# Gated attention and MLP mixer on one core: the spreading of head rows and the split of the output projection rewritten, selection matrices built on another engine

## The chip, the cores and the metric

The kernel runs on one core of one Trainium2 chip. Its time is device microseconds (us) from the start to the end of one launch. The profile is one execution of the same program on that core; its span runs from the first instruction to the last. Engines are named as in the profile: PE is the matrix engine (PEld its weight loads), DVE the vector engine, ACT the scalar engine, POOL is GpSimd, and SP is the engine whose queue issues the large transfers (DMA).

## The reference

Eight sequences with one new token each (x is 8 x 448, bf16). Two branches are mixed by a gate, out = g * a + (1 - g) * b:

```python
g = sigmoid((x * gate_w).sum(-1, keepdims=True))
# a: 16 query heads of 256 over 8 cached KV heads, last 1024 positions of 4096
q = (x @ wq).reshape(B, Sq, Hq, Dh).transpose(0, 2, 1, 3)
scores = einsum("bhqd,bhkd->bhqk", q, k) * (Dh ** -0.5)
o = einsum("bhqk,bhkd->bhqd", softmax(scores), v)
a = o.transpose(0, 2, 1, 3).reshape(B, Sq, Hq * Dh) @ wo      # (8, 4096) @ (4096, 448)
# b: an MLP
h = gelu(layernorm(x) @ w1 + b1)
b = h @ w2 + b2
```

The caches that are read (1024 positions of K and of V, 8 heads, 8 sequences) are 67 MB, the weights some 11 MB.

## The kernel before, in words

All large transfers go through one SP queue into a ring of 9 slots of 2 MB (`RING`, `pump`, `done`). Their order is a fixed plan: wq, the first K block, w1, w2, then K and V blocks by turns, the last two V blocks, and at the end wo in four pieces: quarters 0 and 1 in one (1792 KB), quarter 2 (896 KB), six eighths of quarter 3 (672 KB), and the rest of it (224 KB). A slot is loaded again when its reader is done. The order of instructions on each engine is the order in which the Python code writes them; semaphores between engines are placed automatically, tile by tile.

**Start.** POOL fills constants, the last of them `qw` (line 290, a memset of 128 x 5120). DVE builds small selection matrices out of the identity matrix `ident`, among them `pick` (lines 282 to 289): four copies of 128 x 128. Then the norm and the gate are computed (`norm_and_gate`; POOL fills `each` at line 337), then the query (`query`): wq matmuls into `Sq`, ACT scales them to bf16, PE transposes them, DVE arranges them into `qd`, PE multiplies by the four matrices in `pick` (line 393) into a two-bank PSUM tile `qp`, and ACT (line 406) and DVE (line 408) by turns copy blocks of 32 rows of `qp` into `qw`: ACT the half j = 0, DVE the half j = 1, for each of four row blocks.

**Loop.** A unit u (16 of them) is one sequence and four KV heads. DVE transposes the K block in two halves (line 351), PE makes scores (lines 417 and 423), DVE takes maxima, ACT exponentiates, DVE transposes the result back, PE multiplies by V (line 495), ACT and DVE pick out the own heads, and `finish(u)` (lines 525 and 528) puts the gated attention output, transposed, into columns of `oT`. In the iterations u = 12, 13 and 14, `keep_clock(idle, 2, 1)` (line 636) adds three matmuls whose result nobody reads: one in f32 and two in bf16, each 512 columns wide.

**End.** `oT` holds, for partition p, head h, half j and batch b, the attention output at head dimension 2p + j. The projection wants on each partition eight consecutive rows of wo, so `spread_rows` regroups: PE multiplies four strided column picks of `ident` (32 columns each) by four groups of heads, 16 matmuls of 64 columns, each into its own 32 rows of the PSUM tile `pp` (line 660), and DVE copies the whole of `pp` into `oP` (line 667). `oP` is cut into four quarters q of 8 blocks j. The product with wo is accumulated over q and j. Quarters 0 and 1 are done in whole rows of 448 columns (`project_whole`, line 673) into `A_all`, which already holds the MLP part (`begin`); ACT copies `A_all` to SBUF (`save_whole`, line 683). Quarters 2 and 3 are done in two halves of 224 columns (`project`, line 701) into two PSUM tiles that sit on different rows (0 to 7 and 32 to 39). Between them, `add_whole` (line 687) adds the saved rows to the halves by f32 matmuls with an identity. DVE (line 744) and ACT (line 745) write the two halves of `res`, and one DMA (line 746) stores it. `keep_clock(spare, ...)` puts matmuls that nobody reads between the steps of this stage.

Of the kernel before, what the change touches and what calls it, by code (L numbers as in the profile page):

```python
# [12 lines left out]
F32 = mybir.dt.float32  # L13
# [5 lines left out]
def kernel(  # L19
# [15 lines left out]
    nc = tc.nc  # L35
    P = nc.NUM_PARTITIONS

    NB, Sq, D = A_x.shape
# [8 lines left out]
    NJ = Dh // P  # L47
# [9 lines left out]
    QUAD = 4  # L57
    RQ = QUAD * rep
    NQ = NB * Hkv // QUAD
# [6 lines left out]
    HPQ = 4  # L66
    NHQ = Hq // HPQ
# [3 lines left out]
    NK = 4  # L71
    NPAR = 2
    KP = NK * NPAR
    BLK = 32
# [12 lines left out]
    ps_s = ctx.enter_context(tc.tile_pool(name="ps_s", bufs=2, space=PSUM))  # L87
    ps_sm = ctx.enter_context(tc.tile_pool(name="ps_sm", bufs=2, space=PSUM))
# [13 lines left out]
    def done(n=1):  # L102
        consumed[0] += n
        pump()
# [72 lines left out]
    def slot(*key):  # L177
        return slots[index[key]]
# [18 lines left out]
    ident = consts.tile([P, P], BF16)  # L197
# [20 lines left out]
    pick = consts.tile([P, NK // NJ, NPAR, P], BF16)  # L218
# [60 lines left out]
        place[:],  # L279
        ident[:, 0:BLK].rearrange("p (o x) -> p o x", o=1).to_broadcast([P, CH, BLK]),  # L280
    )
    for kk in range(NK // NJ):
        for par in range(NPAR):
            nc.vector.tensor_copy(
                pick[:, kk, par, :].rearrange("p (b w) -> p b w", b=QUAD),
                ident[:]
                .rearrange("p (k o w r) -> p k r o w", k=NK // NJ, o=1, r=NPAR)[:, kk, par]
                .to_broadcast([P, QUAD, BLK]),
            )
    nc.gpsimd.memset(qw[:], 0.0)  # L290

    def norm_and_gate():
        stats = consts.tile([NB, nc.vector.BN_STATS_DIM], F32)
# [53 lines left out]
    def turn_keys(u, hf):  # L347
        kn = slot("k", u)
        kt = ktpool.tile([P, CH, NK, BLK, NPAR], BF16, tag="kt", name="kt")
        KT[u, hf] = kt  # L350
        nc.vector.transpose(  # L351
            kt[:].rearrange("p c k x r -> p (c k x r)").bitcast(WORD),
            kn[:, hf * CH * Dh : (hf + 1) * CH * Dh].bitcast(WORD),
        )
        if hf == NH - 1:
            done()

    def query():
        for r in range(NR + 1):
            w, o = slot("wq", r // 2), (r % 2) * HD  # L360
            for n in range(W // QN):
                for t in range(QUAD):
                    col = t * W + n * QN
                    half, c = divmod(col, HH) if r == NR else (0, col)
                    nc.tensor.matmul(  # L365
                        Sq[32 * t : 32 * t + NB, n * QN : (n + 1) * QN],
                        lhsT=xT[:, r + half, :],
                        rhs=w[:, o + c : o + c + QN],
                        start=(r == 0),
                        stop=(r == NR),  # L370
                        skip_group_check=True,
                    )
        done(2)
        qs = epool.tile([P, W], BF16, tag="E", name="qs")
        nc.scalar.activation(qs[:], Sq[:], ACT.Copy, scale=qscale)
        qt = ps_sm.tile([P, HPQ, NJ, P], BF16, tag="sm", name="qt")
        for hh in range(HPQ):
            for j in range(NJ):
                o = (hh * NJ + j) * P
                nc.tensor.transpose(qt[:, hh, j, :], qs[:, o : o + P], ident[:])  # L380
        qd = consts.tile([P, NJ, NB, 2, 2, HPQ], BF16)
        for j in range(NJ):
            for half in range(2):
                nc.vector.tensor_copy(  # L384
                    qd[:, j, :, half],
                    qt[:, :, j, 64 * half : 64 * half + 64]
                    .rearrange("p h (q b) -> p b q h", q=2)[:, 0:NB],
                )
        qp = ps_s.tile([P, NJ, NU, QUAD, RQ], F32, tag="S", name="qp")
        for j in range(NJ):  # L390
            for kk in range(NK // NJ):
                for par in range(NPAR):
                    nc.tensor.matmul(
                        qp[:, j, :, kk * NPAR + par, :],
                        lhsT=pick[:, kk, par, :],
                        rhs=qd[:, j].rearrange("p b h q i -> p (b h) (q i)"),
                        start=True,
                        stop=True,
                    )
        for b in range(QUAD):  # L400
            rows = slice(BLK * b, BLK * (b + 1))
            for j in range(NJ):
                dst = qw[rows, j, :, BLK * b : BLK * (b + 1)]
                src = qp[rows, j].rearrange("p u m q -> p u (m q)")
                if j == 0:
                    nc.scalar.copy(dst, src)  # L406
                else:
                    nc.vector.tensor_copy(dst, src)  # L408

    S = {}  # L410

    def scores(u, hf):
        if hf == 0:
            S[u] = ps_s.tile([P, W], F32, tag="S", name="S")
        cols = slice(hf * CH * BLK, (hf + 1) * CH * BLK)
        kt = KT.pop((u, hf))
        nc.tensor.matmul(  # L417
            S[u][:, cols], lhsT=foreign[:], rhs=place[:], start=True, stop=False
        )
        for k in range(NK):  # L420
            for par in range(NPAR):
                j, m = k // (NK // NJ), k % (NK // NJ) * NPAR + par
                nc.tensor.matmul(  # L423
                    S[u][:, cols],
                    lhsT=qw[:, j, u, m * RQ : m * RQ + P],
                    rhs=kt[:, :, k, :, par],
                    start=False,
                    stop=(k == NK - 1 and par == NPAR - 1),
                )
# [178 lines left out]

    norm_and_gate()
    query()  # L610
    for hf in range(NH):
        turn_keys(0, hf)
    hs = mlp_hidden()
# [4 lines left out]
    for u in range(1, NQ):  # L618
        turn_keys(u, 0)
        scores(u, 0)  # L620
        if u >= LAG + 1:
            gather(u - LAG - 1)
        if u >= LAG:
            turn(u - LAG)
            total(u - LAG)
        if u >= LAG + 1:
            finish(u - LAG - 1)
        top(u - 1)
        share(u - 1)
        turn_keys(u, 1)  # L630
        if u >= LAG:
            values(u - LAG)
            invert(u - LAG)
        scores(u, 1)
        if NQ - 4 <= u < NQ - 1:
            keep_clock(idle[:], 2, 1)
        expo(u - 1)
    u = NQ - 1
# [4 lines left out]
    oP = consts.tile([P, NJ8, NHQ, NB], BF16)  # L643
    oTv = oT[:].rearrange("p (q i) j b -> p i j q b", i=HPQ)
# [9 lines left out]
        )  # L654

    def spread_rows():
        pp = ps_sm.tile([P, HPQ, NJ, NHQ, NB], F32, tag="sm", name="pp")
        for i in range(HPQ):
            for m in range(HPQ):
                nc.tensor.matmul(  # L660
                    pp[32 * i : 32 * i + 32, m],
                    lhsT=ident[:, m::HPQ],
                    rhs=oTv[:, i],
                    start=True,
                    stop=True,
                )
        nc.vector.tensor_copy(oP[:], pp[:].rearrange("p m j q b -> p (m j) q b"))

    def project_whole(q):
        w = slot("wo", q - q % 2)  # L670
        for j in range(NJ8):
            o = ((q % 2) * NJ8 + j) * D
            nc.tensor.matmul(  # L673
                whole,
                lhsT=oP[:, j, q, :],
                rhs=w[:, o : o + D],
                start=False,
                stop=False,
                skip_group_check=True,
            )  # L680

    def save_whole():
        nc.scalar.copy(mixb[:], whole)

    def add_whole():
        for i, dst in enumerate(halves):
            nc.tensor.matmul(
                dst,
                lhsT=ident_f[:],
                rhs=mixb[:, i * DH2 : (i + 1) * DH2],  # L690
                start=False,
                stop=False,
                skip_group_check=True,
            )

    def project(q):
        w = slot("wo", q - q % 2)
        for j in range(NJ8):
            o = ((q % 2) * NJ8 + j) * D
            for i, dst in enumerate(halves):  # L700
                nc.tensor.matmul(  # L701
                    dst,
                    lhsT=oP[:, j, q, :],
                    rhs=w[:, o + i * DH2 : o + (i + 1) * DH2],
                    start=(q == HALF and j == 0),
                    stop=(q == NHQ - 1 and j == NJ8 - 1),
                    skip_group_check=True,
                )

    HALF = NHQ // 2  # L710
    gather(u - 2)
    finish(u - 2)
    turn(u - 1)
# [21 lines left out]
    A_hi = ps_sm.tile([P, DH2], F32, tag="sm", name="A_hi")  # L735
    halves += [spare[0:NB, 0:DH2], A_hi[32 : 32 + NB, :]]
    project_whole(0)
    project_whole(1)
    save_whole()
    project(2)  # L740
    add_whole()
    project(3)

    nc.vector.tensor_copy(res[:, 0:DH2], halves[0])  # L744
# [32 lines left out]
```

## Time and profile before

| what | value |
|---|---|
| time, median of 4 runs | 191.88 us (191.27 to 193.57) |
| time of the profiled execution | 191.44 us |
| its span | 189.0 us |
| around the span | 191.44 - 189.0 = 2.44 us |
| mean granted PE clock | 0.925 |
| PE, DVE, ACT, POOL busy | 134.0, 126.7, 46.8, 6.5 us |
| bytes moved | 77.81 MB, mean 412 GB/s |
| large-transfer queue busy | 96.6% of 16 engines' span |

In the rows shown further down, a timeline row gives the start in us from the span's beginning, the duration in us, the engine, the source line, the operation, the tile that is written and (after the arrow) those that are read, the count, and in brackets how long the engine had been idle and what released it. A row with a count above one covers several instructions from the first's start to the last's end. A group row gives busy time and mean ns of one, then the idle time ahead of the group and its releasers. A row of windows gives a stretch, then the busy time and count of each engine, the granted PE clock (1.00 is full), the busy share of the DMA engines and GB/s.

### The profile page before, as it was taken

To read this page: it belongs to the slowest core of one execution; us is meant where nothing else is said; L and a number is where in the kernel's file an instruction comes from. 1 tells how busy PE (TensorE), PEld (TensorE's weight loads), DVE (VectorE), ACT (ScalarE), POOL (GpSimd) and SP (SyncE) were. 2 spreads that over 40 slices of the span, in tenths; PEclk is the share of its full clock that TensorE was granted. 3 is DMA by queue.
4 is the path that set the end of the run, shared out by engine and by line. 5 is a ranking of instruction groups with operands and counts; after the bars stand their busy time and mean duration, and the time that the engine had idled before them with its cause. 6 is when DMAs were issued, how large, how long until landed. Compare 5 with 4: busy or idle time off the path is not lost.

```text
span 189.0 us, 2171 instructions
## 1 busy us (share of the span) xinstructions
PE 134.0 (71%) x854; PEld 63.0 (33%) x854; DVE 126.7 (67%) x175; ACT 46.8 (25%) x95; POOL 6.5 (3%) x15
## 2 busy tenths in 40 slices
PE   0027609998758998675759684979396969698994
PEld 0012203444424343423324331534152424245342
DVE  2850489999949494949494949595867677685200
ACT  3032330134040404040404040224040403135201
POOL 8500000000000000000000000000000000000000
PEclk9999657999996579999969998899999999999998
DMA  5999999999999999999999999999999999999990
GB/s 192 415 444 410 434 446 421 423 440 433 423 433 433 427 437 420 433 440 430 420 428 437 433 433 423 423 440 437 423 420 444 437 420 430 427 440 436 400 372 9
DMA packets 6315, 77.81 MB, mean 412 GB/s; under 512 B 841, under 2 KB 994, under 8 KB 1698
## 3 DMA queue, kind: packets, MB, share of 16 engines
q1 hardware_dynamic: 6128, 77.67, 96.6%
q8 instruction: 6, 0.10, 0.2%
q10 hardware_dynamic: 178, 0.02, 0.1%
q14 instruction: 3, 0.02, 0.0%
HBM read 77.68 MB, written 0.01 MB: 411 GB/s over the span
## 4 chain that ended last, share of the span: by engine, by line
DMA 64%; PE 17%; DVE 13%; ACT 4%; issue 1%; SPq 0%; ACTq 0%; DVEq 0%
DMA slot<-in_A_k_cache_dram 61%; DVE kt L351 5%; PE S L423 5%; DMA x_sb<-in_A_x_dram 2%; PE Sq L365 2%; PE A_all L673 2%; DVE qw L408 1%; PE bb L591 1%; ACT qw L406 1%; DVE mx L435 1%; DVE xz L243 1%; PE PO L495 1%; PE A_lo L605 1%; PE A_lo L701 1%; PE fin L525 1%
## 5 line engine op out<-in xcount | busy, mean ns | idle before, releaser
L351 DVE STREAM_TRANSPOSE kt<-slot 128x2048 int32<-128x2048 int32 x32 | 73.7, 2306 | 31.3 <-DMA slot<-in_A_k_cache_dram 31.3
L423 PE MATMUL S<-kt,qw 128*128 128x512 bf16 x256 | 67.5, 409 | 31.8 <-DVE kt L351 31.3
L423 PEld LDWEIGHTS <-qw 128*128 128x128 bf16 x256 | 26.0, 102 | 70.0 <-issue 45.2
L528 ACT ACTIVATE oT<-fin,gg_s 128x16 bf16<-128x16 f32 x16 | 5.2, 328 | 75.5 <-PE fin L525 75.5
L452 ACT ACTIVATE E<-S,nmx 128x1024 bf16<-128x1024 f32 x16 | 22.3, 1391 | 1.9 <-DVE nmx L449 1.8
L435 DVE TENSOR_REDUCE mx<-S 128x1 f32<-128x1024 f32 x16 | 19.0, 1190 | 0.3 <-PE S L423 0.2
L495 PE MATMUL PO<-slot,ET 128*16 128x512 bf16 x256 | 17.5, 395 | 0.3 <-DMA slot<-in_A_v_cache_dram 0.3
L504 ACT ACTIVATE first<-PO,own 128x256 f32<-128x256 f32 x16 | 7.6, 473 | 26.9 <-PE PO L495 25.7
L417 PE MATMUL S<-place,foreign 128*128 128x512 bf16 x32 | 12.9, 402 | 0.1
L465 DVE STREAM_TRANSPOSE ET<-E 128x512 int32<-128x512 int32 x16 | 11.2, 697 | 2.2 <-ACT E L452 2.2
L443 PE MATMUL mz<-m,same 128*128 128x4 f32 x32 | 6.2, 265 | 5.6 <-ACT oT L528 5.5
L476 PEld LDWEIGHTS den<-rowsum,rowden 128*128 128x128 f32 x32 | 6.4, 206 | 3.4 <-ACT oT L528 0.8
L443 PEld LDWEIGHTS mz<-m,same 128*128 128x128 f32 x32 | 5.0, 195 | 7.5 <-ACT oT L528 6.6
L495 PEld LDWEIGHTS <-ET 128*16 128x16 bf16 x256 | 5.1, 89 | 5.3 <-DVE rb L486 0.8
L417 PEld LDWEIGHTS <-foreign 128*128 128x128 bf16 x32 | 3.2, 100 | 9.1 <-issue 7.6
L487 ACT ACTIVATE rsel<-sel,rb 128x8 f32<-128x8 f32 x16 | 4.7, 292 | 1.2 <-DVE rb L486 1.2
L476 PE MATMUL den<-rowsum,rowden 128*128 128x1 f32 x32 | 4.9, 222 | 0.0
L408 DVE CAST qw<-qp 32x512 bf16<-32x512 f32 x4 | 2.7, 687 | 3.1 <-ACT qw L406 3.1
L290 POOL MEMSET qw<- 128x5120 bf16 x1 | 4.4, 4354 | 0.0
L437 DVE TENSOR_SCALAR m<-block,mx 128x4 f32<-128x4 f32 x16 | 3.7, 229 | 0.6
L744 DVE CAST res<-A_lo 8x224 bf16<-8x224 f32 x1 | 0.4, 379 | 5.4 <-PE A_hi L701 5.4
L384 DVE COPY qd<-qt 128x64 bf16<-128x64 bf16 x4 | 0.6, 217 | 5.0 <-PE qt L380 5.0
(152 smaller groups left out, 98.9 us busy)
## 6 DMA issues: line engine op xcount, KB each, us to landing
slot<-in_A_k_cache_dram SPq DMA_DIRECT2D x16, 2048.0 KB, 36.2
slot<-in_A_v_cache_dram SPq DMA_DIRECT2D x16, 2048.0 KB, 36.7
slot<-in_A_wq_dram SPq DMA_DIRECT2D x1, 2048.0 KB, 7.8
slot<-in_A_wo_dram SPq DMA_DIRECT2D x1, 1792.0 KB
slot<-in_B_w_dram SPq DMA_DIRECT2D x1, 1568.0 KB
slot<-in_B_w_dram SPq DMA_DIRECT2D x1, 1344.0 KB, 11.8
slot<-in_A_wq_dram SPq DMA_DIRECT2D x1, 1024.0 KB, 9.8
slot<-in_A_wo_dram SPq DMA_DIRECT2D x1, 896.0 KB, 33.5
```

The costliest lines, as they stand in the source:

```text
L351: nc.vector.transpose(kt[:].rearrange("p c k x r -> p (c k x r)").bitcast(WORD), kn[:, hf * CH * Dh : (hf + 1) * CH * Dh].bitcast(WORD),)
L417: nc.tensor.matmul(S[u][:, cols], lhsT=foreign[:], rhs=place[:], start=True, stop=False)
L423: nc.tensor.matmul(S[u][:, cols], lhsT=qw[:, j, u, m * RQ : m * RQ + P], rhs=kt[:, :, k, :, par], start=False, stop=(k == NK - 1 and par = ...
L435: nc.vector.reduce_max(mx[:], S[u][:], axis=AXIS.X)
L443: nc.tensor.matmul(mz[:], lhsT=same[:], rhs=m4[:], start=True, stop=True)
L452: nc.scalar.activation(E[:].rearrange("p c x i -> p c i x"), S.pop(u)[:].rearrange("p (c i x) -> p c i x", i=PAIR, x=BLK), ACT.Exp, bias=n ...
L465: nc.vector.transpose(ET[:].rearrange("p c r i -> p (c r i)").bitcast(WORD), E[:].rearrange("p c x i -> p (c x i)").bitcast(WORD),)
L476: nc.tensor.matmul(den[u][:], lhsT=rowden[:], rhs=rowsum[:], start=True, stop=True)
L487: nc.scalar.activation(rsel[u][:], sel2[:], ACT.Copy, scale=rb[:])
L495: nc.tensor.matmul(PO[32 * t : 32 * t + PAIR * RQ], lhsT=ET[:, c, 0:RQ, :], rhs=vn[:, PAIR * c * Dh : PAIR * (c + 1) * Dh], start=(c < QUA ...
L504: nc.scalar.activation(first[:], PO[:, 0, :], ACT.Copy, scale=own[:, 0:1])
L528: nc.scalar.activation(oT[:, half * RQ : (half + 1) * RQ, :, b].rearrange("p h j -> p j h"), sm[:], ACT.Copy, scale=gg_s[:, b : b + 1],)
```

## The change

1. **`pick` on POOL.** The four DVE copies go. POOL makes all of `pick` in one copy of 128 x 512 elements, after its memset of `qw`.
2. **`pick` used twice.** After `query()`, POOL overwrites the same memory with another selection matrix, `spreader`: four matrices of 128 x 128, in each of which a set of 32 identity columns (every fourth one) is repeated four times.
3. **`spread_rows`.** Instead of 16 matmuls of 64 columns with 32-column weights there are 4 matmuls of 256 columns with 128-column weights. Each row block of the result now holds all four groups of heads, and the wanted one is picked when `pp` is copied: four copies of 32 rows, blocks 0 and 2 by DVE, blocks 1 and 3 by ACT. `pp` is now two PSUM banks (128 x 1024 f32) and comes from the pool of the score tiles.
4. **Projection.** Only quarter 0 is done in whole rows; quarters 1, 2 and 3 in halves. The saved rows are added after quarter 1 in place of after quarter 2.
5. **Filler.** The three unread matmuls of iteration u = 12 go; those of 13 and 14 stay.

```diff
-    for kk in range(NK // NJ):
-        for par in range(NPAR):
-            nc.vector.tensor_copy(
-                pick[:, kk, par, :].rearrange("p (b w) -> p b w", b=QUAD),
-                ident[:]
-                .rearrange("p (k o w r) -> p k r o w", k=NK // NJ, o=1, r=NPAR)[:, kk, par]
-                .to_broadcast([P, QUAD, BLK]),
-            )
     nc.gpsimd.memset(qw[:], 0.0)
+    nc.gpsimd.tensor_copy(
+        pick[:].rearrange("p k r (b w) -> p k r b w", b=QUAD),
+        ident[:]
+        .rearrange("p (k o w r) -> p k r o w", k=NK // NJ, o=1, r=NPAR)
+        .to_broadcast([P, NK // NJ, NPAR, QUAD, BLK]),
+    )
...
     query()
+    spreader = pick[:].rearrange("p a b m -> p (a b) m")
+    nc.gpsimd.tensor_copy(
+        spreader.rearrange("p m (b x) -> p m b x", b=HPQ),
+        ident[:]
+        .rearrange("p (x o m) -> p m o x", o=1, m=HPQ)
+        .to_broadcast([P, HPQ, HPQ, BLK]),
+    )
...
-        if NQ - 4 <= u < NQ - 1:
+        if NQ - 3 <= u < NQ - 1:
             keep_clock(idle[:], 2, 1)
...
     def spread_rows():
-        pp = ps_sm.tile([P, HPQ, NJ, NHQ, NB], F32, tag="sm", name="pp")
+        pp = ps_s.tile([P, HPQ, HPQ, NJ * NHQ * NB], F32, tag="S", name="pp")
+        for m in range(HPQ):
+            nc.tensor.matmul(
+                pp[:, m], lhsT=spreader[:, m], rhs=oTv, start=True, stop=True
+            )
+        ov = oP[:].rearrange("p (m j) q b -> p m (j q b)", m=HPQ)
         for i in range(HPQ):
-            for m in range(HPQ):
-                nc.tensor.matmul(
-                    pp[32 * i : 32 * i + 32, m],
-                    lhsT=ident[:, m::HPQ],
-                    rhs=oTv[:, i],
-                    start=True,
-                    stop=True,
-                )
-        nc.vector.tensor_copy(oP[:], pp[:].rearrange("p m j q b -> p (m j) q b"))
+            rows = slice(BLK * i, BLK * (i + 1))
+            if i % 2 == 0:
+                nc.vector.tensor_copy(ov[rows], pp[rows, :, i])
+            else:
+                nc.scalar.copy(ov[rows], pp[rows, :, i])
...
-    def project(q):
+    def project(q, first=False):
...
-                    start=(q == HALF and j == 0),
+                    start=(first and j == 0),
...
     project_whole(0)
-    project_whole(1)
     save_whole()
+    project(1, first=True)
+    add_whole()
     project(2)
-    add_whole()
     project(3)
```

More of the change, by code (lines that the diff above doesn't have):

```diff
@@ L708, in project @@
                 )
-    HALF = NHQ // 2
     gather(u - 2)
```

## The prediction

> **What bounds the kernel now.** I read the busy lines and the slices of the page first, then the windows, the DMA issues, and the timeline of the last ten microseconds; the timeline of the query came last, because it holds the nearest relatives of the new copies.
>
> The slices say that the transfer queue is the limit for nearly the whole span:
>
> ```profile
> PE   0027609998758998675759684979396969698994
> DVE  2850489999949494949494949595867677685200
> ...
> PEclk9999657999996579999969998899999999999998
> DMA  5999999999999999999999999999999999999990
> ```
>
> The reader is to see that DMA stands at 9 from the second slice to the last but one, while PE and DVE breathe. Until the last V block and wo have landed, a saving on PE or DVE moves nothing. The windows show where that ends:
>
> ```profile
> 180.00:185.00 5.00, 4.96 (x53) 2.48 (x54) 0.42 (x1) 0.60 (x2) 0.00 (x0) 1.00 0.77 318
> 185.00:189.00 4.00, 1.37 (x21) 0.69 (x20) 0.38 (x1) 0.34 (x1) 0.00 (x0) 0.87 0.01 4
> ```
>
> PE is busy 4.96 of 5.00 us from 180 to 185 at a granted clock of 1.00, and the DMA share falls from 0.77 to 0.01. The issues of wo by themselves: quarter 2 goes out at 149.63 and takes 33.5 us to land, so 183.13; six eighths of quarter 3 at 152.43 plus 32.4, so 184.83; the rest at 157.31 plus 28.0, so 185.31. Thus the last nine microseconds are a serial chain on PE, with the transfers close behind it:
>
> ```profile
> 179.75 0.33 ACT L528 ACTIVATE oT<-fin,gg_s 128x16 bf16<-128x16 f32 x1 [1.25 <-PE fin L525]
> 180.13 0.37 PE L660 MATMUL pp<-oT,ident 128*32 128x64 bf16 x16
> 180.43 0.60 PE L607 MATMUL A_lo<-place,foreign 128*128 128x512 bf16 x2
> 180.56 0.42 DVE L667 CAST oP<-pp 128x256 bf16<-128x256 f32 x1 [1.54 <-PE pp L660]
> 181.08 2.81 PE L673 MATMUL A_all<-slot,oP 128*8 128x448 bf16 x14
> 184.30 0.52 ACT L683 COPY mixb<-A_all 8x448 f32<-8x448 f32 x1 [4.22 <-PE A_all L673]
> 184.96 0.35 PE L687 MATMUL A_lo<-mixb,ident_f 8*8 8x224 f32 x1
> 186.41 0.38 DVE L744 CAST res<-A_lo 8x224 bf16<-8x224 f32 x1 [5.42 <-PE A_hi L701]
> ```
>
> Call T0 the start of the projection, 181.08 here; PE's last matmul ends at 186.42, T0 + 5.34.
>
> **The change part by part.**
>
> *Projection.* The 16 whole-row matmuls start 0.189 us apart ((183.91 - 181.08) / 15). A pair of halves starts every 0.0935 us (seven pairs of quarter 3 from 185.44 to 186.11, counted with the eighth). So quarter 1 goes from 8 x 0.189 = 1.51 to 8 x 0.0935 = 0.75 us. The new wait is that of PE for the saved rows: now `A_all` ends at 184.26 and the addition starts at 184.96, 0.70 later, covered by quarter 2 but for 0.20. Afterwards: whole quarter 0 ends at T0 + 7 x 0.189 + 0.35 = T0 + 1.67, the addition can start at T0 + 2.37; quarter 1 issues from T0 + 1.51 to T0 + 2.26. PE idles 0.11, with quarters 2 and 3 queued behind it. The addition takes 0.48 (184.96 to 185.44), so quarter 2 starts at T0 + 2.85, quarter 3 at T0 + 3.60, and with 0.98 for it (185.44 to 186.42) PE ends at T0 + 4.58. Gain 0.76 us, on the path.
>
> *Spread matmuls.* 16 of 64 columns, 0.37 in all, become 4 of 256. Their step lies between rows of 128 columns (line 380: 8 in 0.62, 0.057 apart) and 512 (line 423: 8 in 1.90 with 0.39 for the last, 0.216 apart): 0.108, and 0.27 for the last, 3 x 0.108 + 0.27 = 0.60. Ends: 4 of the 128-column row, 3 x 0.057 + 0.22 = 0.39, and 4 of the 512-column row, 3 x 0.216 + 0.39 = 1.04. I take 0.60, +0.23. The filler behind it moves along and ends near 181.2, still ahead of the projection.
>
> *The four copies.* One takes 256 elements per partition as line 667 did, so DVE 0.42 each (ends: 0.38 of line 744 with 224, 0.69 of line 408 with 512). ACT: line 745 has 0.336 for 224 and line 406 0.576 for 512; in between, 0.36 (those are the ends). Whether they run side by side decides the sign. Two ACT/DVE groups in this kernel answer it: at the end, lines 744 and 745 read two PSUM tiles and start 0.03 us apart. In the query, lines 406 and 408 read one PSUM tile, and they take turns, though each reads its own half:
>
> ```profile
> 20.47 0.57 ACT L406 CAST qw<-qp 32x512 bf16<-32x512 f32 x1 [1.86 <-PE qp L393]
> 21.07 0.68 DVE L408 CAST qw<-qp 32x512 bf16<-32x512 f32 x1 [1.14 <-ACT qw L406]
> ...
> 21.79 0.58 ACT L406 CAST qw<-qp 32x512 bf16<-32x512 f32 x1 [0.75 <-DVE qw L408]
> ...
> 22.40 0.68 DVE L408 CAST qw<-qp 32x512 bf16<-32x512 f32 x1 [0.64 <-ACT qw L406]
> ```
>
> Each starts 0.03 to 0.04 us after the other engine's end, and the trace names that engine as releaser, also between different row blocks (21.75 to 21.79). The new copies have the same pattern, blocks of 32 rows of one PSUM tile taken by DVE and ACT by turns, so I take them as serial: 0.42 + 0.04 + 0.36 + 0.03 + 0.42 + 0.04 + 0.36 = 1.67 in place of 0.42, +1.25. The handoff from the last one to PE is 0.14 when ACT is last (184.82 to 184.96) against 0.10 now, +0.04. Sum with the spread: T0 moves by 0.23 + 1.25 + 0.04 = +1.52. At the low ends of all three it is +1.52 - 0.21 - 0.12 = +1.19, at the high ends +1.52 + 0.44 + 0.98 = +2.94.
>
> A rule of the Trainium skill speaks for the other case. "PSUM — Partial Sum Buffer", section "PSUM bank collisions raise a hardware error", says that two engines may read one bank at the same time as long as they are in different groups of 32 partitions, which is exactly how the new copies divide `pp`. By that rule DVE and ACT would work side by side and the sum would be that of the first rival below. But the row shows what this program's semaphores do, not what the memory allows, and it decides.
>
> *Net on the path.* +1.52 - 0.76 = +0.76 us.
>
> *`pick` on POOL.* DVE loses four copies, 0.53 on the chain at 9.07. POOL gets a copy of the size of `place` (line 278, 0.60 us), starting at 6.88; ends 0.30 (line 209, a memset of half the elements) and 4.35 (line 290). Behind it on POOL is only `each` (line 337, 0.30), which DVE wants at 13.16; PE wants `pick` at 19.07. Even at 4.35 both are there. POOL can also hold up DVE: the two copies of line 243 took 2.08 us, until POOL's memset had ended, where one copy of that size is 0.20 at line 308. That could cost the DVE copies near 8 us up to the length of the new copy. So the query moves by -0.5 to +3.8 us. What hides it: the first nine slots are 17.4 MB, 40 us of transfers at 430 GB/s, and the first of them comes free with the query at 17.5. The queue has over 20 us of work at that point. Zero at the end.
>
> *`spreader`.* One more POOL copy, after PE's last read of `pick` (20.38), wanted at 180: nothing waits. Zero.
>
> *Filler of u = 12.* It filled PE from 141.66 to 143. Without it PE idles some 3.0 us until 145.09. The kernel has such gaps: 2.96 us before 135.35, after which the clock stayed at 1.00, and 2.98 before 115.91, after which it fell to 0.50 and eight matmuls took 3.22 in place of 1.90. So the cost is 0 or some 1.7 us at 145, where PE next waits for K by over 1.7 us; the transfer queue covers it. Zero at the end, as the fillers of 13 and 14 stay.
>
> *Sum.* The profiled execution's 191.44 + 0.76 = 192.20. It lies 0.44 below the median; on the median of 191.88 the forecast is 192.64, call it 192.6.
>
> **The rivals.**
>
> *Copies side by side.* Then DVE's two bound the stage, 0.42 + 0.34 (a second one without its overhead, from line 384: 4 in 0.62 where one is 0.217, so each further one saves 0.08) = 0.76 in place of 1.67, and DVE hands over last. T0 moves by 0.23 + 0.34 = +0.57, the net is -0.19: 191.7. For it: different row blocks, and lines 744 and 745. Against it: lines 406 and 408.
>
> *The clock falls in the last stage.* While the copies run, PE has nothing from 181.2 to 182.6, 1.4 us. If that made the clock fall to half, as before 115.91, PE's remaining work (8 x 0.189 + 24 x 0.0935 + 0.48 = 4.24 us) would take up to twice that: 191.88 + 0.76 + up to 4.2, at most 196.9. It makes the kernel slower by over 1% from 1.2 us of such work at half clock. Against it: gaps of 1.76 us before 145.09 and 2.96 before 135.35 left the clock at 1.00, and PE is busy 4.96 of 5.00 ahead of this one.
>
> *A gain above 1%.* The last piece of wo lands at 185.31; after it come two pairs of matmuls, 0.19 + 0.26, so PE can't end before 185.76, 0.66 ahead of today. More than 0.7 us can only come from the transfer stream itself, of which the change touches nothing: its share is 0.88 or more in every window that I read between 4 and 180, and 1.01 over the whole of that stretch. Price of the whole floor: 191.2.
>
> **How the numbers follow.** Serial copies 0.72, side by side 0.14, fallen clock 0.09, faster stream or floor 0.05. About 1% (1.9 us) is what a measurement of this kernel can tell from no change. Serial with all unknown costs at their ends gives 191.88 + 1.19 - 0.76 = 192.3 to 191.88 + 2.94 - 0.76 = 194.1; the side-by-side case adds 191.7, and the scatter of the runs (0.6 below the median) takes it to 191.2 at the bottom. The range is 191.2 to 193.9. Over 1% slower (193.8): the clock case and the upper end of the serial case with the scatter, 0.19. Over 1% faster: 0.05. Within: 0.76.
>
> **What would show it.** Four copies each starting as the other engine's ends; spread matmuls in some 0.60 us; the projection at 182.6; PE ending 4.58 us after it; the wait before the addition at 0.1; the clock at 1.00 to the end. Copies that overlap, or a time under 191, would make me wrong; so would an end that moved by more than the shift of T0 less 0.76.

## The result and the profile after

| | before | after |
|---|---|---|
| time, median | 191.43 us (79 runs) | 192.18 us (53 runs) |
| ratio, with 95% interval | | 1.0038 (1.0025 to 1.0050) |
| span of the profiled execution | 189.0 us | 189.9 us |
| last `oT` done to start of the projection | 180.08 to 181.08: 1.00 us | 180.29 to 182.68: 2.39 us |
| start of the projection to DVE's copy of the result | 181.08 to 186.41: 5.33 us | 182.68 to 187.27: 4.59 us |

The change makes the kernel 0.4% slower, 0.0038 x 191.43 = 0.73 us. That is within 1%, but clear of zero. The last two rows of the table, one profiled execution each, split it: the spreading loses 1.39 us, the projection wins 0.74.

The slices of the page after. PE's last slice but one is 7 where it was 9. DMA's is 7 for 9 too, but only because that slice lies 0.9 us later (from 180.4 to 185.2 in place of 179.6 to 184.3), nearer to the end of the transfers:

```profile
PE   0027609998758866665769985978499969698974
...
DMA  6999999999999999999999999999999999999970
```

The windows of the last ten microseconds of the kernel after say the same in numbers: PE busy is 3.68 of 5.00 us where it was 4.96, DVE's two copies and ACT's two are there, and the granted clock (the third figure from the end) is 1.00 in both stretches:

```profile
180.00:185.00 5.00, 3.68 (x32) 1.88 (x30) 0.83 (x2) 1.53 (x4) 0.00 (x0) 1.00 0.76 313
185.00:190.00 5.00, 2.23 (x38) 1.47 (x36) 0.38 (x1) 0.34 (x1) 0.00 (x0) 1.00 0.01 5
```

The timeline of that stage after, to be laid beside the one of before:

```profile
179.96 0.33 ACT L526 ACTIVATE oT<-fin,gg_s 128x16 bf16<-128x16 f32 x1 [1.25 <-PE fin L523]
180.33 0.60 PE L664 MATMUL pp<-oT,pick 128*128 128x256 bf16 x4
180.97 0.41 DVE L671 CAST oP<-pp 32x256 bf16<-32x256 f32 x1 [1.74 <-PE pp L664]
181.41 0.36 ACT L673 CAST oP<-pp 32x256 bf16<-32x256 f32 x1 [1.13 <-DVE oP L671]
181.81 0.42 DVE L671 CAST oP<-pp 32x256 bf16<-32x256 f32 x1 [0.43 <-ACT oP L673]
182.26 0.36 ACT L673 CAST oP<-pp 32x256 bf16<-32x256 f32 x1 [0.49 <-DVE oP L671]
182.68 1.30 PE L679 MATMUL A_all<-slot,oP 128*8 128x448 bf16 x6 [1.32 <-ACT oP L673]
184.40 0.52 ACT L689 COPY mixb<-A_all 8x448 f32<-8x448 f32 x1 [1.77 <-PE A_all L679]
185.06 0.35 PE L693 MATMUL A_lo<-mixb,ident_f 8*8 8x224 f32 x1
187.27 0.38 DVE L749 CAST res<-A_lo 8x224 bf16<-8x224 f32 x1 [5.04 <-PE A_hi L707]
```

The four copies are a staircase: each starts 0.03 to 0.04 us after the one on the other engine has ended, and the bracket names that engine. (It names the releasing instruction by the tile that this instruction writes, `oP`; which tile the wait stands for it does not say, and two experiments below decide that.) PE sits idle for 1.32 us until the last of them. Everything behind 182.68 is shorter than before by what the projection saves.

At the start, the copies of `pick` are gone from DVE, and yet the query begins at the same time, 14.03 against 14.02. The first of these rows is of the kernel before, the others are of the kernel after; they say why:

```profile
4.90 2.08 DVE L243 COPY xz<-x_sb 8x64 bf16<-8x64 bf16 x2 [2.42 <-DMA x_sb<-in_A_x_dram]
...
2.53 4.36 POOL L282 MEMSET qw<- 128x5120 bf16 x1
4.96 2.58 DVE L243 COPY xz<-x_sb 8x64 bf16<-8x64 bf16 x2 [2.48 <-DMA x_sb<-in_A_x_dram]
6.84 0.60 POOL L283 COPY pick<-ident 128x512 bf16<-128x512 bf16 x1
...
14.03 3.41 PE L363 MATMUL Sq<-slot,xT 128*8 128x512 bf16 x32
```

Two small DVE copies, 2.08 us long before, are now 2.58 us long: they end at 7.54, after POOL's new copy, in place of 6.98, after POOL's memset. DVE pays in longer copies what it saves by leaving `pick` to POOL.

### The profile page after: what moved, and what is told of

Its sections match the earlier page's. It is cut to its first block, busy times and chain, and to the rows that moved or that the text cites. A ratio compares the mean times of both kernels' runs of the same rounds, so it can differ in the third digit from the quotient of the medians.

```text
span 189.9 us, 2157 instructions
## 1 busy us (share of the span) xinstructions
PE 134.7 (71%) x846; PEld 63.9 (34%) x846; DVE 127.0 (67%) x172; ACT 47.5 (25%) x97; POOL 7.7 (4%) x17
## 4 chain that ended last, share of the span: by engine, by line
DMA 84%; PE 8%; DVE 3%; ACT 2%; SPq 1%; issue 0%; ACTq 0%
DMA slot<-in_A_k_cache_dram 84%; PE A_lo L707 1%; DVE kt L349 1%; PE PO L493 1%; PE A_lo L603 1%; PE S L421 1%; PE A_all L679 1%; PE fin L523 1%; ACT E L450 1%; SPq L131 1%; DVE mx L433 1%; DVE oP L671 0%; ACT first L502 0%; PE A_all L652 0%; ACT oP L673 0%
## 5 line engine op out<-in xcount | busy, mean ns | idle before, releaser
L421 PE MATMUL S<-kt,qw 128*128 128x512 bf16 x256 | 68.7, 414 | 30.6 <-DVE kt L349 30.1
L493 PE MATMUL PO<-slot,ET 128*16 128x512 bf16 x256 | 18.3, 410 | 0.3 <-DMA slot<-in_A_v_cache_dram 0.3
L474 PEld LDWEIGHTS den<-rowsum,rowden 128*128 128x128 f32 x32 | 6.9, 220 | 3.8 <-issue 1.1
L243 DVE COPY xz<-x_sb 8x64 bf16<-8x64 bf16 x2 | 2.6, 2504 | 2.5 <-DMA x_sb<-in_A_x_dram 2.5
L447 DVE TENSOR_REDUCE nmx<-mz 128x1 f32<-128x4 f32 x16 | 2.3, 145 | 2.8 <-PE mz L441 2.8
```

The lines of the kernel that those rows point to most:

```text
L421: nc.tensor.matmul(S[u][:, cols], lhsT=qw[:, j, u, m * RQ : m * RQ + P], rhs=kt[:, :, k, :, par], start=False, stop=(k == NK - 1 and par = ...
L474: nc.tensor.matmul(den[u][:], lhsT=rowden[:], rhs=rowsum[:], start=True, stop=True)
L493: nc.tensor.matmul(PO[32 * t : 32 * t + PAIR * RQ], lhsT=ET[:, c, 0:RQ, :], rhs=vn[:, PAIR * c * Dh : PAIR * (c + 1) * Dh], start=(c < QUA ...
```

## The experiments

The theory was the prediction's: the copies take turns because they read one PSUM tile, the projection's saving is real, and the start is hidden behind the transfers. The rivals: the turns come from something else, the transfers hide the saving, the early edits matter. The kernels ran in three groups, each group on one chip with the kernel before beside it, and ratios are to that. The first group is two tiles, projection alone, spreading alone and early edits undone; the third is one tile, all copies on DVE and the last pair; the rest is the second. Beside the ratios I give the median span over all executions, less that of before in the same group (189.1, 189.5 and 189.2 us in the three groups), since it leaves out what lies around the span.

**Two PSUM tiles.** Each engine has a tile of its own.

```diff
+        pa = ps_sm.tile([P, 2, HPQ, NJ * NHQ * NB], F32, tag="sm", name="pa")
+        pb = ps_s.tile([P, 2, HPQ, NJ * NHQ * NB], F32, tag="S", name="pb")
...
+            nc.vector.tensor_copy(ov[rows, 0:2], pa[rows, :, i])
+            nc.scalar.copy(ov[rows, 2:4], pb[rows, :, i])
```

> The changed kernel, but the wide products 0 and 1 go to one PSUM tile that only DVE reads and products 2 and 3 to another that only ACT reads; each engine makes four copies of 32 x 128 into its own columns of oP. Theory (the turns come from reading one PSUM tile): the engines overlap; DVE needs about 0.29 + 3 x 0.20 = 0.9 us, ACT about the same and starts 0.2 later, so the projection starts some 0.85 us earlier than in the changed kernel, and the time is about that of before (ratio 0.999). Rival (the turns come from writing one SBUF tile, oP): eight copies by turns, 4 x (0.29 + 0.04 + 0.26 + 0.03) = 2.5 us in place of 1.7, 0.8 us slower than the changed kernel, ratio to before about 1.008.

Ratio 1.0003 (0.9981 to 1.0025), span +0.05 us. The timeline of this kernel (four copies per row):

```profile
181.91 1.19 DVE L672 CAST oP<-pa 32x128 bf16<-32x128 f32 x4 [1.53 <-PE pa L666]
182.13 1.06 ACT L673 CAST oP<-pb 32x128 bf16<-32x128 f32 x4 [0.69 <-PE pb L666]
183.15 1.04 PEld L679 LDWEIGHTS <-oP 128*8 128x8 bf16 x7 [1.13 <-DVE oP L672]
```

DVE and ACT overlap for nearly the whole of their time, though both write `oP` (each its own columns). The projection starts 1.71 us after `oT` (181.44 to 183.15) in place of 2.39. That is 0.68 won where 0.85 was expected; the copies follow each other at 0.30 us, not 0.20. The rival (turns from the writes to `oP`) falls.

**The same copies, one PSUM tile.** Only the allocation differs from the kernel just shown: `pp` is one tile of two banks, DVE reads only the first bank and ACT only the second.

```diff
-        pa = ps_sm.tile([P, 2, HPQ, NJ * NHQ * NB], F32, tag="sm", name="pa")
-        pb = ps_s.tile([P, 2, HPQ, NJ * NHQ * NB], F32, tag="S", name="pb")
+        pp = ps_s.tile([P, HPQ, HPQ, NJ * NHQ * NB], F32, tag="S", name="pp")
...
-            nc.vector.tensor_copy(ov[rows, 0:2], pa[rows, :, i])
-            nc.scalar.copy(ov[rows, 2:4], pb[rows, :, i])
+            nc.vector.tensor_copy(ov[rows, 0:2], pp[rows, 0:2, i])
+            nc.scalar.copy(ov[rows, 2:4], pp[rows, 2:4, i])
```

> The two-tile kernel again with one thing undone: the four wide products go to one PSUM tile of two banks, and DVE reads only its first bank, ACT only its second; the copies, their sizes and their order are those of the two-tile kernel. Theory (the turns belong to the PSUM tile): the eight copies take turns, 4 x (0.29 + 0.04 + 0.26 + 0.03) = 2.5 us from first to last in place of 1.2, and the time is 1.3 us above the two-tile kernel, ratio to before about 1.007. Rival (what counts is the bank or the 32 rows): they overlap as with two tiles, ratio about 1.000.

Ratio 1.0072 (1.0039 to 1.0106), span +1.15 us, 1.1 more than with two tiles. In the profiled execution the granted clock was down in several stretches ahead of these rows (0.50 from 176.8 to 180.3 is the last of them), and `oT` is done late, at 182.89; at the rows themselves the clock was back at 1.00 (the first five of the eight copies and the last):

```profile
183.57 0.28 DVE L670 CAST oP<-pp 32x128 bf16<-32x128 f32 x1 [1.74 <-PE pp L664]
183.88 0.26 ACT L671 CAST oP<-pp 32x128 bf16<-32x128 f32 x1 [1.00 <-DVE oP L670]
184.17 0.28 DVE L670 CAST oP<-pp 32x128 bf16<-32x128 f32 x1 [0.32 <-ACT oP L671]
184.49 0.26 ACT L671 CAST oP<-pp 32x128 bf16<-32x128 f32 x1 [0.35 <-DVE oP L670]
184.77 0.29 DVE L670 CAST oP<-pp 32x128 bf16<-32x128 f32 x1 [0.32 <-ACT oP L671]
...
185.71 0.26 ACT L671 CAST oP<-pp 32x128 bf16<-32x128 f32 x1 [0.36 <-DVE oP L670]
```

Same copies, same sizes, same order, and now they take turns: 183.57 to 185.97, 2.40 us in place of about 1.3, and the projection starts 2.85 us after `oT` (182.89 to 185.74) in place of 1.71. Banks and rows are divided alike in the two kernels, so it is the shared tile that sets the turns here, by the semaphores that are placed between DVE and ACT. This is the pair of runs that carries the study's main point. Not tried is the other half: whether writing different rows of `oP`, as the changed kernel does, would bring turns by itself with two PSUM tiles.

**All copies on DVE.**

```diff
-            if i % 2 == 0:
-                nc.vector.tensor_copy(ov[rows], pp[rows, :, i])
-            else:
-                nc.scalar.copy(ov[rows], pp[rows, :, i])
+            nc.vector.tensor_copy(ov[rows], pp[rows, :, i])
```

> The changed kernel with all four copies out of the wide product on DVE. Theory (in turns, ACT's two copies win nothing): four copies on one engine need about 4 x 0.42 = 1.7 us, at best 0.42 + 3 x 0.34 = 1.4, so the time is that of the changed kernel or up to 0.3 us less, ratio to before 1.002 to 1.004. Rival (ACT carried half of the work): about 0.8 us more, ratio 1.008.

Ratio 1.0041 (1.0008 to 1.0074), span +0.75 us.

```profile
180.97 1.72 DVE L670 CAST oP<-pp 32x256 bf16<-32x256 f32 x4 [1.75 <-PE pp L664]
```

Four DVE copies take 1.72 us, from 180.97, and PE starts 2.46 us after `oT`, against 2.39 with ACT's help. Two engines in turns are here worth hardly more than one (0.07 us). The lower of my two figures, 1.4, was wrong: these copies do not overlap each other, 1.72 / 4 = 0.43 each.

**Projection alone.** The kernel before, with only the order of quarters and the sums changed.

```diff
     project_whole(0)
-    project_whole(1)
     save_whole()
+    project(1, first=True)
+    add_whole()
     project(2)
-    add_whole()
     project(3)
```

> The kernel before with the new projection alone: quarter 0 in whole rows, quarters 1 to 3 in halves; spreading, selection matrices and filler as before. Theory: the projection starts at 181.1 as before and PE ends 4.6 us after it in place of 5.3, 0.66 to 0.75 us earlier, just where the last piece of wo (landing near 185.3) allows it: ratio to before about 0.9963. Rival (the transfers hide it): the wait moves to the last piece of wo and the time stays, ratio 1.000.

Ratio 0.9990 (0.9964 to 1.0015), span -0.5 us. The time alone leaves both answers open; the span and the profile say that the saving is there and where it ends. PE's weight loads for quarters 2 and 3 (17 of them in the first row: quarter 2 and one of quarter 3):

```profile
184.12 0.76 PEld L701 LDWEIGHTS <-oP 128*8 128x8 bf16 x17 [0.38 <-issue]
185.06 0.67 PEld L701 LDWEIGHTS <-oP 128*8 128x8 bf16 x15 [0.19 <-issue]
```

Quarter 3 stops and goes on at 185.06. Its first piece of wo was issued at 152.65 and took 32.4 us to land: 185.05. The page names "issue" for the gap, since the release did not show, but the landing fits to 0.01 us. So the gain is cut by about 0.18 us, by the transfers.

**Spreading alone.** The changed kernel with the old projection (the diff just shown, backwards).

> The changed kernel with the projection as it was before: quarters 0 and 1 in whole rows. Theory: the terms add, so the projection starts 1.4 to 1.5 us late and nothing is won back: ratio to before about 1.0075. Rival (part of the late start is given back, because the transfers would have held PE up anyway): under 1.005.

Ratio 1.0075 (1.0050 to 1.0099), span +1.5 us; 2.40 us from `oT` to the projection (180.35 to 182.75). The terms add, and nothing is given back.

**Early edits undone.** `pick` by DVE again, and the filler of u = 12 back; spreading and projection stay changed.

> The changed kernel with pick made by four DVE copies again and the unread matmuls of u = 12 back, that is spreading and projection alone. Theory: both edits are hidden behind the transfer queue, so the time is that of the changed kernel, ratio to before 1.0035 to 1.004. Rival (the 0.2 us that all of the last stage is late in the profile of the changed kernel, ahead of the first new instruction there, comes from these two edits): 0.2 us less, ratio about 1.0025.

Ratio 1.0073 (1.0039 to 1.0106): outside both expectations. Five of eleven executions had spans of 190.9 to 192.6, the other six 189.7 to 190.1, which is 0.6 to 1.0 above before, as in the changed kernel, so the rival's 0.2 us does not show in them either. The profiled execution is one of the five, and its rows show what happens there:

```profile
175.24 1.10 PE L605 MATMUL A_lo<-qw,same 128*128 128x512 f32 x2
176.84 1.84 PE L495 MATMUL PO<-slot,ET 128*16 128x512 bf16 x16 [0.49 <-DMA slot<-in_A_v_cache_dram]
178.60 1.98 PE L605 MATMUL A_lo<-qw,same 128*128 128x512 f32 x2
```

The same two f32 matmuls take 1.98 us at 178.60 and 1.10 at 175.24; the granted clock in the windows is 0.73 from 176 to 178 and 0.50 from 178 to 180. `oT` is done at 181.31, over 1 us late; from there on all is as in the changed kernel (2.40 us to the projection, at 183.71). The two-tile and the one-tile kernels had the same spell in their profiles.

**Filler back, nothing else** (`NQ - 4 <= u` again in the changed kernel).

> The changed kernel with the three unread matmuls of u = 12 back and nothing else. It asks why the kernel with both early edits undone was over 1 us longer in five of eleven executions (spans of 190.9 to 192.6 against 189.8), with a granted clock of 0.50 to 0.73 between 176 and 180 in its profile. Theory (the filler shifts which stretch the clock gate sees, so it makes that spell commoner): again several of the executions with spans 1 us or more above the rest. Rival (chance, or the other edit): spans as in the changed kernel, at most one in eight above 190.8.

Ratio 1.0029 (1.0000 to 1.0058); two of twelve spans above 190.8 (191.0 and 191.3), the rest 189.5 to 190.4. Two of twelve is a little over the rival's one in eight, but in this group five of the 35 executions of before lie above 190.8 as well. So nothing here shows that the filler makes long spans common, and it does not make the kernel faster or slower by what can be seen.

**The changed kernel again**, beside the last and the next two.

> The changed kernel as it is, beside the others on one chip. Theory: ratio to before 1.004, the projection some 1.4 us later after the last oT than in the kernel before, and 4.6 us long in place of 5.3.

Ratio 1.0028 (0.9998 to 1.0057), span +0.6 us, one of twelve above 190.8. From `oT` to the projection 2.40 us (180.23 to 182.63), and 4.58 from there to DVE's copy of the result.

**A late start.** POOL fills `qw` three times ahead of `pick`.

```diff
     nc.gpsimd.memset(qw[:], 0.0)
+    nc.gpsimd.memset(qw[:], 0.0)
+    nc.gpsimd.memset(qw[:], 0.0)
     nc.gpsimd.tensor_copy(
```

> The changed kernel with the POOL memset of qw done three times in place of once, so pick, the query and the first scores come some 8.7 us later. Theory (the transfer queue has over 20 us of work in hand, so the start is hidden): the time is that of the changed kernel within 0.3 us. Rival (the start is on the path through the release of the slots, as the chain of waits draws it): up to 8.7 us slower, ratio to before up to 1.05.

Ratio 0.9998 (0.9966 to 1.0030), span +0.4 us. The query starts at 20.82 in place of 14.03 and the first K block is turned at 32.57 in place of 25.70, 6.9 us later (not 8.7: DVE's copies ended with the first memset here), and the last `oT` is done at 180.31 against 180.29. The windows of the late start:

```profile
4.00:10.00 6.00, 0.46 (x5) 0.28 (x5) 4.88 (x7) 0.00 (x0) 5.94 (x2) 1.00 1.00 418
10.00:20.00 10.00, 0.45 (x4) 0.28 (x4) 8.71 (x20) 1.78 (x3) 6.43 (x4) 1.00 1.01 429
20.00:30.00 10.00, 6.55 (x67) 2.81 (x67) 2.33 (x8) 2.27 (x4) 0.65 (x1) 1.00 1.03 439
30.00:40.00 10.00, 5.01 (x16) 1.96 (x17) 8.35 (x10) 2.27 (x4) 0.00 (x0) 0.66 1.00 428
```

The DMA share stays at 1.00 or more (the figure before the last) while PE, between 4 and 20, is busy for under a microsecond. Seven microseconds at the start cost nothing, so the half microsecond that moving `pick` could have won was worth nothing either.

**All quarters in halves.** The kernel before without whole rows: the MLP rows open the halves, ahead of the projection.

```diff
-    begin()
...
-    project_whole(0)
-    project_whole(1)
-    save_whole()
+    add_whole()
+    project(0)
+    project(1)
     project(2)
-    add_whole()
     project(3)
```

> The kernel before with all four quarters in halves: the MLP rows open the two halves (by the f32 matmuls of add_whole, while PE waits for oP anyway), and there is no whole-row product, no save and no later addition. By PE's own instructions the projection would be 4 x 0.75 + 0.2 = 3.2 us in place of 5.3, 2.1 us less. Theory (the landing of wo is the floor, reached already by the projection-only kernel, where PE resumed at 185.06 with the piece that was issued at 152.65 and took 32.4): PE waits for the pieces of wo and ends no earlier than in the projection-only kernel, ratio to before 0.997 to 0.998. Rival (PE is the limit to the end): 0.989.

Ratio 0.9944 (0.9917 to 0.9971), span -0.65 us. PE's rows for the last matmul of quarters 1 and 2 and the first one of quarters 2 and 3:

```profile
183.59 0.26 PE L673 MATMUL A_lo<-slot,oP 128*8 128x224 bf16 x1
...
184.04 0.26 PE L673 MATMUL A_lo<-slot,oP 128*8 128x224 bf16 x1 [0.19 <-DMA slot<-in_A_wo_dram]
...
184.71 0.26 PE L673 MATMUL A_lo<-slot,oP 128*8 128x224 bf16 x1
...
185.67 0.26 PE L673 MATMUL A_lo<-slot,oP 128*8 128x224 bf16 x1 [0.69 <-DMA slot<-in_A_wo_dram]
```

Now the profile names the transfer. Issued at 150.46 plus 33.5 is 183.96, at 153.27 plus 32.4 is 185.67: PE goes on 0.08 and 0.00 us after its piece has landed. By the sum in the expectation PE's own instructions are 2.1 us shorter than before, and the span is 0.65 shorter: the floor holds, and the rival (0.989) falls. One detail differs from the expectation: the opening matmuls start at 181.68, as DVE's copy into `oP` ends at 181.70, so they do not fill a wait but put the projection off to 182.15; PE waits for wo behind it for longer than that. The time's ratio is below what I expected, its interval is not.

**The same again, and the slow spreading with it.** Once more the halves-only kernel, and beside it the changed kernel with all quarters in halves.

> The halves-only kernel (spreading, selection matrices and filler as before) again, beside the others on one chip. Theory: ratio to before 0.994 to 0.998.

> The changed kernel with all four quarters in halves, opened by the MLP rows, without whole rows, save and later addition: the slow spreading together with the projection that only waits for wo. Theory (the last piece of wo is the floor): the projection starts at 182.6 and PE's own 3.2 us end at 185.8, where the last piece allows it, so the 1.4 us that the spreading loses are swallowed by the wait for wo: within 0.3 us of the halves-only kernel, ratio to before about 0.997. Rival (the late start adds in full): 1.4 us above the halves-only kernel, ratio 1.002 or more.

Halves only: 0.9942 (0.9921 to 0.9964), span -0.65 us. Slow spreading with halves: 0.9987 (0.9957 to 1.0016), the same median span, 188.55 us. Its projection starts 2.40 us after `oT` (179.90 to 182.30), and quarter 3 goes on at 184.75, its piece having landed at 152.34 + 32.4 = 184.74 (49 weight loads of PE for quarters 0 to 2 and the first of quarter 3, then the other fifteen):

```profile
182.30 2.29 PEld L679 LDWEIGHTS <-oP 128*8 128x8 bf16 x49 [1.29 <-ACT oP L661]
184.75 0.67 PEld L679 LDWEIGHTS <-oP 128*8 128x8 bf16 x15 [0.16 <-issue]
```

So within the span the 1.4 us lost in the spreading are swallowed whole by the wait for wo. The times differ more than the spans, because the part around the span is 2.06 us in the one and 1.81 in the other (medians).

The halves-only kernel beats the kernel before by 0.6% in both groups, and the changed kernel in the group where that ran beside it (0.9944 against 1.0028).

## Why the prediction was right, point by point

- **The four copies in turns: right.** This term decided the sign. It was read from the query's copies of before, and the one-tile and two-tile kernels show that the reason was right too: sharing one PSUM tile is enough for turns. Measured, first start to last end: 180.97 to 182.62, 1.65 us for 1.67 predicted. The page of the Trainium skill that I weighed against it, "PSUM — Partial Sum Buffer", section "PSUM bank collisions raise a hardware error", allows two engines on one bank in different groups of 32 partitions. The two-tile kernel gives each engine a bank of its own and so does not try that; the one-tile kernel shows that here the semaphores, not the banks, decide.
- **Spread matmuls: right.** 0.60 predicted, 0.60 measured.
- **The last handoff to PE: too dear.** 0.14 predicted, 182.62 to 182.68 measured, 0.06. Together the start of the projection moved by 1.39 against `oT`, not 1.52. This is the only term of the shift that was off by more than 0.03 us.
- **Projection: right.** 0.76 predicted, 0.74 measured. The prediction's step for a pair of halves is a little short: 185.44 to 186.11 is seven steps of 0.096, not 0.0935. With 0.096 its own sum gives 0.74. The wait ahead of the addition came out as expected: counted in the same way, quarter 1's last pair makes room at 184.20 + 8 x 0.096 = 184.97 and the addition starts at 185.06, 0.09 us later. (The row of PE's loads gives 0.19 for it, as it gave 0.20 before.)
- **The sum: right, and its closeness in part luck.** 0.76 predicted; 1.39 - 0.74 = 0.65 in the stage, 0.73 in the time. That the time comes nearer to the forecast than the stage does is not owed to any term. The 192.6 us were counted from a median of before of 191.88 in four runs; over 79 runs it is 191.43, and the kernel after came to 192.18. The stage began 0.2 us later than in the profile of before (179.96 against 179.75 for the last `oT`), but the projection-only kernel, which has the old start, shows the same 179.95, so the change is not needed to explain it; each is one profile. The part around the span has a median of 2.0 us in the changed kernel and 1.9 over 97 executions of before in the three groups; whether that 0.1 belongs to the change is open.
- **The early edits: right.** The query moved by 0.01 us: the gain of 0.53 on DVE was eaten by its two copies of line 243, which ended only after POOL's new copy had (7.54 against 7.44), and not by the DVE copies near 8 us, where I had expected it. The late-start kernel shows that 6.9 us would have been hidden too.
- **Side by side: too cheap.** Had the copies overlapped, two of 0.43 would have made 0.86, not 0.76, since copies out of PSUM in this shape do not overlap on one engine (four took 1.72).
- **The fallen clock: wrong in its place.** I put it into PE's new gap and made it hang on gaps of some 3 us. The gap of 1.32 us left the clock at 1.00. The spell that three of the profiles show comes ahead of it, at 176 to 180.
- **The floor: right**, to 0.01 us at quarter 3 in three kernels. I used it only to bound a gain; it is also what limits the best version.

## What to carry to other kernels

In this program, splitting a copy out of PSUM between two engines helped only when each read a tile of its own. Look in the profile for a pair that already shares one, and see whether the second starts before the first ends. In a kernel whose transfers end late, compare each consumer's start with issue plus landing of its piece before counting PE time saved: the smaller of the two is the gain. Work moved off an engine early, while transfers had over 20 us of work in hand, was worth nothing here, and came back as a wait for the engine that took it.

## What the runs showed of the hardware that was not expected

The granted clock fell to 0.50 for some 3.4 us late in the loop in three profiles: from 176.3 to 179.7 with two tiles, and from about 176.9 to 180.3 with one tile and with the early edits undone. PE had no idle stretch of over 0.5 us in the eight microseconds ahead; the last `oT` came 1.0 us or more later than in the kernel after. The kernel before has gaps of 2.96 and 2.98 us, one with a fall of the clock behind it and one without, and in the kernel after a gap of 2.25 us (ahead of 116.12) has one behind it: 0.53 from 116 to 118. So the length of PE's gaps alone does not tell when the clock falls here. Spans of 1 us or more above the median came in 15 of 97 executions of before (one more, of 679.2 us, is left out) and in 7 of 66 of the changed kernel. With the early edits undone, five of 11 lie that far above the median of the other six (189.8). Whether that is more than chance, and what the long spans have in common, stays open, since only one of the five has a profile.
